# Where to undo a row permutation: in the output store, or in a copy on the way

## The chip, the cores and the metric

The kernel runs on one core of one Trainium2 chip. The metric is the device time in microseconds of one execution; of several executions the median is given. Beside it there is a profile of one execution, which names each instruction by its engine, its source line and the tiles that it reads and writes.

## What is computed

The reference is an attention with a small mask, followed by a feed-forward layer with a maximum of three projections in place of an activation function. All inputs and the output are fp32.

```python
B, H, S, D = 4, 8, 768, 64                  # batch, heads, tokens, head width
scores = q @ k.transpose / sqrt(D)          # keep: the last 96 positions, and the first 8 keys
scores = where(keep, scores - slope[h] * dist, -1e9)
attn   = softmax(scores) @ v                # (4, 8, 768, 64)

x   = attn.transpose(0, 2, 1, 3).reshape(3072, 512)
h   = max(x @ w1, x @ w2, x @ w3)           # 512 -> 768
out = h @ w_out                             # (3072, 512)
```

The kernel cuts the 3072 tokens into 24 tiles of 128 (tile T; six to a batch). Since a query sees only the 96 positions before it, a tile of queries needs its own tile of keys and the one before.

## The kernel before

The whole kernel is one hand-written order of small units, held in a string. A word such as `F0.1.0` calls a unit with its numbers. Each engine works through its own instructions in the order in which the words issue them, and waits where an input is not there yet or a buffer is not free.

- `T` (`u_XT`): the attention result of one tile is transposed, so that the feed-forward layer can multiply it. In `T1.1` the last number says how: 0 copies with ScalarE, 1 with VectorE, 2 with GpSimd, 4 transposes with a DMA.
- `F` (`u_F1`): one of the three up-projections (last number) of one 128-wide block of the hidden width for one chunk of tiles.
- `O` (`u_F2`): the down-projection of one tile (`O0.1.0` is chunk 0, second tile of it, copy by ScalarE) and the store of its 128 output rows.
- `X`: the transpose of queries and keys of one tile (`X18.4` by a DMA); `S`: scores; `A`: probabilities times values; `W`: cast of a weight block; `K`: a mask from an exponential.

The chunks are tiles 0-1, 2-3, 4-5, 6-7, 8-11, 12-15, 16-19, 20-23.

For an early start, the first four tiles of batch 0 are loaded in a way of their own: a partition takes four successive tokens, so that each read is longer. The queries of these tiles stay in that order. Within such a tile, row `e*32 + i` holds the token `4*i + e`. The order runs through scores, probabilities, attention result and feed-forward layer, and the output store of these tiles undoes it:

```python
    copies = (nc.scalar.copy, nc.vector.tensor_copy, nc.gpsimd.tensor_copy)
    # ... cut ...
    def u_XT(T, how):
        # ... cut: xT, the destination of the chunk ...
        dst = xT[B][:, :, lo:lo + 128]                      # [128, 4, 128] bf16
        if how == 4:
            nc.sync.dma_start_transpose(out=dst, in_=xb[T].rearrange("p h d -> p (h d)"))
            return
        if early(T):                                        # T < 4
            tp = psH.tile([128, NP, 128], BF16, name="xtp", tag="h")
        else:
            tp = psT.tile([128, NP, 128], BF16, name="xtp", tag="tp")
        x = xb[T].rearrange("p h d -> p (h d)")
        for jp in range(NP):
            nc.tensor.transpose(tp[:, jp], x[:, jp * 128:(jp + 1) * 128], identb)
        copies[how](dst, tp)

    def u_F1(c, f, j):
        # ... cut ...
        ps = psH.tile([128, W], FP32, name="h", tag="h")    # psH has three buffers
        for dm in range(4):
            nc.tensor.matmul(ps, w123[f // 2][:, dm, j, (f % 2) * 128:(f % 2) * 128 + 128],
                             xT[B][:, dm, o], start=(dm == 0), stop=(dm == 3))
        # ... cut: h01s[c, f] ...
        if j == 0:
            nc.scalar.copy(h01, ps)
        elif j == 1:
            nc.vector.tensor_max(h01, h01, ps)
        else:
            nc.vector.tensor_max(ht[B][:, f, o], h01, ps)

    def f2_out(po, c, tt, copy, cols=slice(0, DM), dma=nc.sync):
        T = chunks[c][tt]
        ost = ost_pool.tile(list(po.shape), FP32, name="ost", tag="ost")
        copy(ost, po)
        rows = out[T * 128:(T + 1) * 128, cols]
        dma.dma_start(out=rows.rearrange("(i e) c -> e i c", e=4) if T < 4 else rows, in_=ost)
```

Another unit, `u_x`, copies transposed queries and keys and has the same choice between a straight and a strided copy (lines 256 and 259 of the kernel):

```python
            if n == 0 and a == 0:
                copy(batch_T(0)[:, 0, j0 + lo:j0 + hi, 0:sz * 128].rearrange("c j (e i) -> c j e i", e=sz),
                     tp.rearrange("c e j i -> c j e i"))
            else:
                copy(dst[:, lo:hi], tp.rearrange("c e j i -> c j i e"))
```

All loads, DMA transposes and nearly all stores are issued by the sync engine, in the order of the schedule. Two parts of the string that matter below:

```
    ... s1.2.0 T0.0 C2.1.2 G3.2 C3.1.1 w0.0.0 W0.0.0 K4 T1.1 V1.2
    W0.1.1 A2.1 V2.2 A3.0 T2.0 F0.0.0 T3.1 V3.2 F0.0.1 w1.0.0 W1.0.2 W2.0.0 F0.1.0 F1.0.0 F1.1.0 F1.4.0
    # ... cut ...
    O3.0.1 F4.0.0 A12.0
    T12.4 F4.2.0 F4.2.1 S13.1 M13.1 S13.0 G12.2 F4.0.1 F4.1.0 F4.1.1 F4.1.2 G13.2 S14.0 C13.1.2 M13.0
    S14.1 M14.1 G14.1 M14.0 F4.4.0 F4.4.1 O0.0.0 C14.1.1 S15.1 M15.1 S15.0 G15.0 F4.4.2 C16.0.2 F4.3.0
    F4.3.1 A13.0 V13.1 T13.4 C19.0.1 F4.2.2 M15.0 O0.1.0 A14.0 V14.1 X18.4 X19.4 F4.3.2 O1.0.1 C15.1.2
    A15.0 T15.4 F4.0.2 F4.5.0 X16.4 T14.0 C17.1.1 L17 L20 F4.5.1 F4.5.2 O4.2.0 v19 O4.1.1 S18.0 S18.1
    M18.1 F5.0.0 C18.1.0 F5.1.0 S19.0 S16.1 ...
```

Of the kernel before, what the change touches and what calls it, by code (L numbers as in the profile page):

```python
# [25 lines left out]
    l0.5 c0.5.1 l0.0 D5.28 K5 D3.9 x0.5.3 l0.4 c0.4.1 K7 K1 g2.1.2 c0.0.0 K6 x0.0.2 x0.4.0 D2.9 g2.0.0  # L26
    s0.0.0 g1.0.1 l0.2 c0.2.2 l0.7 l0.1 c0.7.1 c0.1.1 K3 l0.6 c0.6.2 s1.0.1 v1 l0.3 x0.1.1 s0.1.0 x0.2.1
    g1.1.2 c0.3.2 x0.6.3 s0.2.1 x0.3.3 C1.1.2 g1.2.1 x0.7.2 s0.3.1 g2.3.0 v0 s1.1.0 C0.1.2 A0.2 w0.1.0
    v2 K0 g1.3.2 s1.3.1 G0.2 A1.2 v3 g2.2.2 s1.2.0 T0.0 C2.1.2 G3.2 C3.1.1 w0.0.0 W0.0.0 K4 T1.1 V1.2
    W0.1.1 A2.1 V2.2 A3.0 T2.0 F0.0.0 T3.1 V3.2 F0.0.1 w1.0.0 W1.0.2 W2.0.0 F0.1.0 F1.0.0 F1.1.0 F1.4.0  # L30
    F1.1.1 w0.2.0 l1.0 c1.0.2 F1.2.0 F0.4.0 W0.2.1 F1.0.1 F1.1.2 F0.1.1 F0.0.2 F1.3.0 x1.0.4 F1.0.2 l1.1
    F1.5.0 c1.1.2 x1.1.4 F0.2.0 w1.1.0 W1.1.2 F0.3.0 S4.1 K2 S4.0 G4.2 W2.1.1 F0.1.2 F1.5.1 M4.1 F1.4.1
    S5.1 F0.4.1 M4.0 M5.1 F0.2.1 F0.3.1 S5.0 v4 C4.1.2 A4.1 F0.5.0 F0.5.1 F1.2.1 w1.2.0 W1.2.0 W2.2.2
# [28 lines left out]
def kernel(  # L62
# [122 lines left out]
    copies = (nc.scalar.copy, nc.vector.tensor_copy, nc.gpsimd.tensor_copy)  # L185
# [49 lines left out]
    def early(T):  # L235
        return T < NSTART
# [152 lines left out]
    def u_XT(T, how):  # L389
        c, i = where[T]  # L390
        B = BIG[c]
        if B not in xT:
            xT[B] = xT_pool.tile([128, NP, WBIG[B]], BF16, name="xT", tag="xT")
        lo = OFF[c] + i * 128
        dst = xT[B][:, :, lo:lo + 128]
# [3 lines that stand above are left out]
        if early(T):  # L399
# [3 lines that stand above are left out]
        x = xb[T].rearrange("p h d -> p (h d)")  # L403
        for jp in range(NP):
            nc.tensor.transpose(tp[:, jp], x[:, jp * 128:(jp + 1) * 128], identb)  # L405
        copies[how](dst, tp)

    ht = {}
    h01s = {}
# [31 lines left out]
    def f2_out(po, c, tt, copy, cols=slice(0, DM), dma=nc.sync):  # L441
        T = chunks[c][tt]
        ost = ost_pool.tile(list(po.shape), FP32, name="ost", tag="ost")
        copy(ost, po)  # L444
        rows = out[T * 128:(T + 1) * 128, cols]
        dma.dma_start(out=rows.rearrange("(i e) c -> e i c", e=4) if T < 4 else rows, in_=ost)

    def u_F2(c, tt, how):
        po = psH.tile([128, DM], FP32, name="po", tag="h")
        f2_mm(po, c, tt, range(NF))  # L450
        f2_out(po, c, tt, copies[how])

    def u_E():
        n = len(chunks[last])
        pos = [psH.tile([128, DM], FP32, name="po", tag="h") for _ in range(2)]
        for tt in range(2):
            f2_mm(pos[tt], last, tt, range(NF - 1))
        for tt in range(2):
            f2_mm(pos[tt], last, tt, [NF - 1])
            f2_out(pos[tt], last, tt, nc.scalar.copy)  # L460
        for tt in range(2, n - 1):
            po = psT.tile([128, DM], FP32, name="po", tag="tp")
            f2_mm(po, last, tt, range(NF))
            f2_out(po, last, tt, nc.scalar.copy)
        for lo, hi, copy, dma in ((0, 256, nc.scalar.copy, nc.sync), (256, 384, nc.vector.tensor_copy, nc.sync),
                                  (384, 512, nc.scalar.copy, nc.scalar)):
            po = psH.tile([128, hi - lo], FP32, name="po", tag="h")
            f2_mm(po, last, n - 1, range(NF), slice(lo, hi))
            f2_out(po, last, n - 1, copy, slice(lo, hi), dma)
# [35 lines left out]
    with tc.manual_schedule():  # L505
# [20 lines left out]
        for h in range(4, H):  # L526
# [14 lines left out]

        units = {"l": load_part, "v": load_v, "c": cast_part, "x": u_x, "L": load, "w": load_w, "o": load_wo, "C": cast, "X": u_X, "S": u_S, "s": u_s, "g": u_g, "M": u_M,
                 "A": u_A, "G": put_kg, "V": put_vg, "T": u_XT, "F": u_F1, "W": cast_w,
                 "K": u_K, "Q": cast_wo, "O": u_F2, "E": u_E, "D": u_D}
        for u in SCHEDULE.split():
# [34 lines left out]
```

## Time and profile before

The time is 192.82 us, the median of three executions (192.77 to 194.81). The profiled execution took 192.07 us; 190.3 us of it lie between its first and last instruction, and all times of the profile are counted from that first instruction.

| | busy us | share of the span | instructions |
|---|---|---|---|
| TensorE, matmuls (PE) | 172.1 | 90% | 1654 |
| VectorE (DVE) | 123.3 | 65% | 269 |
| ScalarE (ACT) | 103.8 | 55% | 166 |
| GpSimd (POOL) | 38.9 | 20% | 68 |

TensorE's mean granted clock is 0.980 of full speed. The DMA engines moved 36.06 MB, at a mean of 190 GB/s.

How to read the lines that follow: a line names a source line (L446), an engine, an operation, and tiles as output<-input. SPq is the sync engine's own issuing of DMAs: the length given there is the time it took to issue, and the time to landing is counted from the start of the issue until the data are there. A chain of work is followed back from the last instruction: at each step to what released it, or to the instruction before it on its engine. Of the 13 copies at L406, seven are on ScalarE (593 ns in the middle) and six on VectorE (420 ns).

### The profile page before, as it was taken

Reading aid. Unit: us, or ns where it says so; the run is one execution under the profiler, and the core shown is the slowest. Engines: PE = TensorE matmul, PEld = TensorE weight load, DVE = VectorE, ACT = ScalarE, POOL = GpSimd, SP = SyncE. Lnnn points to the kernel's source line nnn. Section 1 sums busy time; section 2 is a strip of 40 time slices with the busy share of each in tenths; the row PEclk is TensorE's granted clock in tenths of the full one; section 3 lists DMA queues with packets and bytes.
Section 4 is the critical chain, followed back from the end, with each engine's and each line's share of the span. In section 5 each row is a group of like instructions: output and inputs, shape, how many; then the busy total and the mean of one; then the engine's idle time right before and its main releaser. Section 6 shows DMA issues by size and latency. Waiting matters only on the chain.

```text
span 190.3 us, 4220 instructions
## 1 busy us (share of the span) xinstructions
PE 172.1 (90%) x1654; PEld 104.7 (55%) x1654; DVE 123.3 (65%) x269; ACT 103.8 (55%) x166; POOL 38.9 (20%) x68
## 2 busy tenths in 40 slices
PE   7669799899999999999997059999999999999992
PEld 7345588688888866444553024455445455444442
DVE  7355756994899997466974003989836985435620
ACT  4979948939787794467221118544465605232122
POOL 5343443722094024003100001310003100000000
PEclk9999999999999999999999759999999999999999
DMA  5999999999889899986969899599999511720006
GB/s 151 309 277 332 323 335 348 325 288 221 197 276 222 172 212 149 205 233 152 192 85 163 97 170 269 110 207 127 168 217 277 130 27 61 233 98 0 0 9 215
DMA packets 83668, 36.06 MB, mean 190 GB/s; under 512 B 68288, under 2 KB 78400, under 8 KB 83648
## 3 DMA queue, kind: packets, MB, share of 16 engines
q1 hardware_dynamic: 83504, 35.73, 81.4%
q8 instruction: 13, 0.21, 0.6%
q14 instruction: 7, 0.06, 0.1%
q10 hardware_dynamic: 144, 0.07, 0.1%
HBM read 25.17 MB, written 6.29 MB: 165 GB/s over the span
## 4 chain that ended last, share of the span: by engine, by line
PE 75%; DVE 9%; ACT 7%; DMA 5%; issue 2%; POOL 0%; ACTq 0%; POOLq 0%; DVEq 0%
PE h L418 45%; PE po L438 15%; PE sp L293 5%; DMA xT<-xb 4%; PE op L367 3%; DVE P L350 2%; PE tpp L251 2%; ACT P L333 2%; PE op L370 2%; ACT wmask L344 2%; PE xtp L405 1%; DMA out_dram<-ost 1%; DVE ht L431 1%; DVE h01s L429 1%; DVE xb L386 1%
## 5 line engine op out<-in xcount | busy, mean ns | idle before, releaser
L418 PE MATMUL h<-xT,w 128*128 128x256 bf16 (+1 forms) x576 | 103.8, 329 | 8.1 <-DMA xT<-xb 7.0
L418 PEld LDWEIGHTS <-w 128*128 128x128 bf16 x576 | 53.6, 98 | 43.9 <-DMA xT<-xb 7.2
L297 ACT ACTIVATE P<-sp 128x1024 bf16<-128x1024 f32 (+1 forms) x40 | 36.5, 960 | 16.5 <-PE sp L293 16.4
L438 PE MATMUL po<-wo,ht 128*128 128x512 bf16 (+2 forms) x156 | 33.4, 363 | 0.0
L429 DVE TENSOR_TENSOR h<-h,h 128x512 bf16<-128x512 bf16 x24 | 16.4, 684 | 24.5 <-PE h L418 11.9
L427 ACT CAST h<-h 128x512 bf16<-128x512 f32 x24 | 14.1, 587 | 30.2 <-PE h L418 30.0
L350 DVE TENSOR_TENSOR P<-P,wmask 128x1024 bf16<-128x1024 bf16 x34 | 25.2, 753 | 3.6 <-ACT P L297 3.5
L438 PEld LDWEIGHTS <-ht 128*128 128x128 bf16 x156 | 14.3, 98 | 15.1 <-DVE ht L431 0.2
L444 ACT COPY ost<-po 128x512 f32<-128x512 f32 (+2 forms) x17 | 9.4, 557 | 19.9 <-PE po L438 15.0
L431 DVE TENSOR_TENSOR ht<-h,h 128x512 bf16<-128x512 bf16 x24 | 16.3, 681 | 3.2 <-PE h L418 2.5
L367 PEld LDWEIGHTS <-P 128*128 128x128 bf16 x192 | 12.4, 97 | 3.5 <-issue 1.0
L386 DVE TENSOR_TENSOR xb<-op,rz 128x512 bf16<-128x512 f32 x19 | 13.1, 691 | 0.7
L367 PE MATMUL op<-va,P 128*128 128x65 bf16 x160 | 12.6, 193 | 0.2
L293 PE MATMUL sp<-qkT 64*128 64x128 bf16 x296 | 12.0, 218 | 0.9 <-DMA qkT<-qkb 0.9
L444 DVE COPY ost<-po 128x512 f32<-128x512 f32 (+1 forms) x9 | 5.8, 644 | 10.8 <-PE po L438 10.7
L429 DVE TENSOR_TENSOR h01s<-h01s,h 128x256 bf16<-128x256 bf16 x24 | 9.7, 415 | 4.5 <-PE h L418 2.5
L293 PEld LDWEIGHTS <-qkT 64*128 64x128 bf16 x296 | 8.4, 94 | 7.3 <-issue 5.4
L201 POOL CAST va<-rawv 128x512 bf16<-128x512 f32 x12 | 7.8, 652 | 20.9 <-DMA rawv<-in_v_dram 8.6
L427 ACT CAST h01s<-h 128x256 bf16<-128x256 f32 x24 | 8.8, 378 | 4.7 <-PE h L418 4.2
L370 PEld LDWEIGHTS <-P 128*128 128x128 bf16 x160 | 10.5, 97 | 1.2
L431 DVE TENSOR_TENSOR ht<-h01s,h 128x256 bf16<-128x256 bf16 x24 | 9.7, 416 | 2.1 <-PE h L418 1.5
L195 POOL CAST qkp<-rawp 128x1024 bf16<-128x1024 f32 (+1 forms) x10 | 9.7, 972 | 6.0 <-DMA rawp<-in_q_dram 3.0
(85 smaller groups left out, 159.9 us busy)
## 6 DMA issues: line engine op xcount, KB each, us to landing
rawv<-in_v_dram SPq DMA_DIRECT2D x24, 256.0 KB, 5.8
out_dram<-ost SPq DMA_DIRECT2D x23, 256.0 KB, 4.1
wst<-in_moe_w_dram SPq DMA_DIRECT2D x3, 1024.0 KB, 7.7
raw<-in_q_dram SPq DMA_DIRECT2D x12, 256.0 KB, 4.6
raw<-in_k_dram SPq DMA_DIRECT2D x12, 256.0 KB, 5.1
rawp<-in_q_dram SPq DMA_DIRECT2D x4, 512.0 KB, 8.6
rawp<-in_k_dram SPq DMA_DIRECT2D x4, 512.0 KB, 8.6
wst<-in_moe_w_dram SPq DMA_DIRECT2D x3, 512.0 KB, 7.1
```

The costliest lines, as they stand in the source:

```text
L293: nc.tensor.matmul(sp[:, hh, j2, ds], qT(T - ds, 1)[hsl, jp], qT(T, 0)[hsl, jp], start=True, stop=True, skip_group_check=True)
L297: nc.scalar.activation(P[:, :, 0:n], sp.rearrange("p a b d n -> p (a b) d n")[:, :, 0:n], AF.Exp, bias=0.0, scale=scale)
L350: nc.vector.tensor_mul(P, P, wmask[:, g, :, 1:3])
L367: nc.tensor.matmul(o, get_P(T, g, j2, hh, 0), heads(va[T])[:, h], start=True, stop=(t == 0), skip_group_check=True)
L370: nc.tensor.matmul(o, get_P(T, g, j2, hh, 1), heads(va[T - 1])[:, h], start=False, stop=True, skip_group_check=True)
L386: nc.vector.tensor_tensor(out=x4, in0=o4[:, :, :, 0:64], in1=rz[:, :, :, None].to_broadcast([128, 2, 4, D]), op=ALU.mult)
L418: nc.tensor.matmul(ps, w123[f // 2][:, dm, j, (f % 2) * 128:(f % 2) * 128 + 128], xT[B][:, dm, o], start=(dm == 0), stop=(dm == 3))
L427: nc.scalar.copy(h01, ps)
L429: nc.vector.tensor_max(h01, h01, ps)
L431: nc.vector.tensor_max(ht[B][:, f, o], h01, ps)
L438: nc.tensor.matmul(po, ht[BIG[c]][:, f, lo:lo + 128], wo[:, f, cols], start=(f == 0), stop=(f == NF - 1))
L444: copy(ost, po)
```

## The change

The order of rows is put right one stage earlier and no longer in the store. For tiles 0 to 3, the copy of the transposed attention result out of PSUM writes column `e*32 + i` to column `4*i + e`: it reads straight and writes with a step of four bf16 elements. From there on the tokens are in their natural order, and the store of these tiles writes its 128 rows in order, as all the other stores do. The copies of tiles 1 and 3, which VectorE made, go to ScalarE, where those of tiles 0 and 2 already are. Nothing else in the schedule is moved.

```diff
-    v2 K0 g1.3.2 s1.3.1 G0.2 A1.2 v3 g2.2.2 s1.2.0 T0.0 C2.1.2 G3.2 C3.1.1 w0.0.0 W0.0.0 K4 T1.1 V1.2
-    W0.1.1 A2.1 V2.2 A3.0 T2.0 F0.0.0 T3.1 V3.2 F0.0.1 w1.0.0 W1.0.2 W2.0.0 F0.1.0 F1.0.0 F1.1.0 F1.4.0
+    v2 K0 g1.3.2 s1.3.1 G0.2 A1.2 v3 g2.2.2 s1.2.0 T0.0 C2.1.2 G3.2 C3.1.1 w0.0.0 W0.0.0 K4 T1.0 V1.2
+    W0.1.1 A2.1 V2.2 A3.0 T2.0 F0.0.0 T3.0 V3.2 F0.0.1 w1.0.0 W1.0.2 W2.0.0 F0.1.0 F1.0.0 F1.1.0 F1.4.0
@@ u_XT
-        copies[how](dst, tp)
+        if T < 4:
+            copies[how](dst.rearrange("c j (i e) -> c j e i", e=4), tp.rearrange("c j (e i) -> c j e i", e=4))
+        else:
+            copies[how](dst, tp)
@@ f2_out
-        rows = out[T * 128:(T + 1) * 128, cols]
-        dma.dma_start(out=rows.rearrange("(i e) c -> e i c", e=4) if T < 4 else rows, in_=ost)
+        dma.dma_start(out=out[T * 128:(T + 1) * 128, cols], in_=ost)
```

## The prediction

> **What bounds the kernel now.** I read the chain that ended last first: 75% of its time is on TensorE, 9% on VectorE, 7% on ScalarE, 5% on DMA. A chain that is mostly TensorE can only be shortened where TensorE stood still, so I listed that chain in order of time and looked for a long piece that is no computation. There is one (columns: start us, length us, what):
>
> ```profile
> 98.85 1.73 PE h L418 x8
> 100.58 2.60 PE po L438 x12
> ...
> 103.20 0.35 DVE ost L444
> 103.56 7.84 DMA xT<-xb
> 111.39 0.05 issue
> ```
>
> The waits between 100 and 115 us give what TensorE lost there (total us, times, longest):
>
> ```profile
> PE h L418 <- DMA xT<-xb: 7.0, 1, 7.0
> ...
> PE sp L293 <- DMA qkT<-qkb: 0.9, 1, 0.9
> ```
>
> The 7.0 us are the wait of the first up-projection of the second four-tile chunk (schedule word F5.0.0) for the DMA transpose of tile 15 (T15.4). The 0.9 us are scores of tile 18 waiting for X18.4. All these DMAs are issued in order by one queue, that of the sync engine:
>
> ```profile
> 91.87 1.28 SPq L397 DMA_TRANSPOSE xT<-xb  x1
> 93.24 0.59 SPq L446 DMA_DIRECT2D out_dram<-ost  x1
> 93.93 1.35 SPq L397 DMA_TRANSPOSE xT<-xb  x1
> 95.38 1.81 SPq L446 DMA_DIRECT2D out_dram<-ost  x1
> 97.28 5.54 SPq L266 DMA_TRANSPOSE qkT<-qkb  x2
> 102.92 0.54 SPq L446 DMA_DIRECT2D out_dram<-ost  x1
> 103.56 1.26 SPq L397 DMA_TRANSPOSE xT<-xb  x1
> ```
>
> Laid beside the schedule string, these are T12.4, O0.0.0, T13.4, O0.1.0, X18.4 with X19.4, O1.0.1, T15.4. So all three stores in this stretch are stores of tiles 0 to 2, which the change touches; the fourth, O1.1.0, goes out near 78.6 us, where TensorE waits for nothing. T12.4, behind an ordinary store, landed 3.4 us after its issue. T13.4, behind O0.0.0, took 6.4; X18.4, behind O0.1.0, took 6.7; T15.4, behind O1.0.1, took 7.8. The DMA activity shows why. First 99 to 102.5 us, where the touched store O0.1.0 is draining, in 40 slices (busy share in tenths, then GB/s); below it 164 to 169 us, with ordinary stores:
>
> ```profile
> DMA  9221511222333223324222454568999999992223
> GB/s 88 85 59 41 79 26 18 88 88 94 117 94 94 94 56 82 99 99 143 94 94 94 129 132 129 152 164 208 249 313 269 249 214 146 135 88 76 67 76 105
> ```
> ```profile
> DMA  9995699983000799999999993000088989600000
> GB/s 344 328 393 180 158 225 223 213 188 56 2 0 0 279 360 426 344 377 393 361 410 360 426 360 99 0 0 0 0 311 328 442 328 442 230 17 0 0 0 0
> ```
>
> The permuted store plods at about 94 GB/s with two or three tenths of the engines busy, which is four of sixteen; an ordinary one bursts at 328 to 442. 256 KB at 94 GB/s is 2.8 us, against about 0.7 at 380.
>
> **What the skill says.** "DMA: Bandwidth & Descriptors", section on why a DMA increments its semaphore by 16, says that a transfer runs on the largest count up to 16 that divides the slowest dimension of both access patterns. The permuted destination has 4 as its slowest dimension (e), hence four engines; the straight one has 128, hence 16. The trace agrees: 0.30 of the engines at 92 GB/s from 99.4 to 101.2 us. The same page, on queues, rings and completion order, says that each engine consumes its ring in order, so whatever is issued later waits on those four engines; 6.4, 6.7 and 7.8 against 3.4 us to landing agree. "TensorE: Matmul & The Clock Gate", Part 1, says that an idle window of about 3.4 us halves the clock. The trace agrees in kind: granted clock 0.73 from 104.2 to 111.4 us and 0.83 in the 8.6 us after. "VectorE: DVE Perf Modes", on what auto-detection checks, wants step 1 on 16-bit data for the fast mode: the strided 128x512 copy at L259 takes 688 ns on VectorE against 420 at L406, and 590 on ScalarE against 596 there. That is why the strided copies are all put on ScalarE.
>
> **The change, part by part.**
> (1) *Stores.* Four stores keep their 256 KB and 2 KB rows but go to sixteen engines. I re-time the queue. O0.1.0 takes 0.55 us to issue rather than 1.81: done at 95.95. X18.4 and X19.4 take 1.3 each, as undisturbed ones do, rather than 3.0 and 2.4: done at 98.6. O1.0.1's copy ends near 97.1 (VectorE, start 96.45), so its store goes at 98.65 rather than 102.92. T15.4 has its input at 97.98, so it goes at 99.25 rather than 103.56; with 3.4 to 5 us to landing it is there at 102.7 to 104.3. X18.4 lands near 96.0+4.2 = 100.2. TensorE has other work to 103.18, then tile 18's scores for 0.26, and asks for T15.4 at about 103.45. So it waits from 0 to 0.8 us instead of 0.87+7.0: 7.1 to 7.9 us come out of the chain.
> (2) *Clock.* The first eight 512-column matmuls after the stall take 3.30 us, against 1.73 for eight at 98.85. Without a long stall 1.5 us come out too.
> (3) *The copies, early.* Two VectorE copies of 0.42 (T1, T3) become ScalarE copies of 0.60, and T0 and T2 become strided. ScalarE is full there, 4.79 us of the 5 from 20 to 25. In its order T1.0 comes after the weight cast and the mask exponential:
>
> ```profile
> 20.12 1.08 ACT L494 CAST w<-wst 128x1024 bf16<-128x1024 f32 x1
> 21.07 0.91 ACT L344 ACTIVATE wmask<-rbase 128x384 bf16<-128x384 f32 x1
> 21.84 0.61 ACT L406 COPY xT<-xtp 128x512 bf16<-128x512 bf16 x1
> 22.31 0.42 ACT L427 CAST h01s<-h 128x256 bf16<-128x256 f32 x1
> 22.57 1.10 ACT L494 CAST w<-wst 128x1024 bf16<-128x1024 f32 x1
> ```
>
> So T1 runs at 21.85 to 22.45 (it ended at 19.52 on VectorE). The first up-projection F0.0.0 needs tiles 0 and 1 and moves from 21.53 to about 22.5; its ScalarE copy from 22.31 to about 23.15; then T3.0 until 24.05; then the cast W2.0.0 until 24.95, where it ended at 23.67. PSUM tag h has three buffers, so the fourth and fifth up-projections wait for ScalarE copies that start at 24.95 rather than 23.76. That is 0.9 to 1.2 us of delay, on a stretch where TensorE is the chain (22.85 to 28.58 without a break). VectorE's 0.84 us of relief saves nothing there. If writing every fourth element costs ScalarE more than reading with a stride does, four copies grow: for 0.4 us each, another 1.6. No row of the profile shows ScalarE writing such a stride into SBUF. L344, which reads SBUF fp32 with a stride, takes 871 ns for 384 elements, where 512 from PSUM take 596, so a penalty is possible.
> (4) *Sum.* 192.8 - 7.5 - 1.5 + 1.0 = 184.8. I add 0.9 for what comes back later: TensorE reaches the second half 8 us earlier, while the loads of tiles 17 and 20 (issued 107.6 to 113.0) come only some 5 us earlier, and VectorE is busy 8.83 us of the 10 from 120 to 130. Prediction 185.7.
>
> **Rivals.**
> *A: the stall moves rather than goes.* T15.4 now follows two large transposes and a store closely, and DMA is busy 0.9 to 1.2 of 16 engines' time around there; T15.4 may still land at 106, or tile 16's scores wait for X16.4. For it: X16.4 took 7.4 us, and the loads behind it queue. Against: the share counts queueing, and the bytes moved from 104.2 to 111.4 are only 91 GB/s. Half the gain would stay: 188 to 189.
> *B: the early loss wins.* The strided write costs 1.0 us a copy and ScalarE falls 2.5 us behind at 25 us, never recovered since TensorE is the chain thereafter. Against: ScalarE idles 0.5 us at 25.4 and 1.86 us before 28.62. With the full gain later: 187.
> *C: the stores are hidden and the landing times are the transposes' own.* Then only (3) is left: about 193.8. Against: T12.4 and later transposes land in 2.4 to 4.2 us with ordinary stores around, and the low GB/s.
> *D: all of the stall goes and the downstream follows in full:* 183.5.
>
> **Range and chances.** D and the sum with little given back span 183.5 to 186; A, or B in part, 187 to 189. I take 183.0 to 189.0. Faster by 2% means below 189.0; C and a strong A with B would miss it. Faster 0.87, same 0.11, slower 0.02.
>
> **What would show it.** In the profile after: transposes of tiles 13 and 15 and of 18 landing in 3 to 5 us; the SP queue issuing T15.4 near 100 us (plus the early delay); the wait of L418 on xT below 1 us; no dip of the clock near 105 to 115; the seven ScalarE copies at L406 become nine, and the six of VectorE four; F0.0.0 about 1 us later. The prediction is wrong if the touched stores still drain at about 94 GB/s, if T15.4 goes out early and yet lands 7 us later, or if strided copies of 1 us stand in the chain near 22 us.

## The result, and the profile after

The changed kernel takes 187.66 us (median; 186.5 to 188.19), the kernel before 193.72 us in the same measurement (192.77 to 194.81). The ratio is 0.968, with a 95% interval from 0.960 to 0.976. The prediction was 185.7 us in a range from 183.0 to 189.0.

In the profiled execution the span went from 190.3 to 184.7 us. Two things happened, of opposite sign. The stall near 104 us is gone:

Chain of work of the kernel after, in order of time (start us, length us, what):

```profile
100.49 1.73 PE h L421 x8
102.22 0.22 PE xtp L405 x4
102.44 1.73 PE h L421 x8
104.17 0.86 PE po L441 x4
105.03 0.05 issue
105.08 1.67 PE po L441 x7
106.75 0.33 PE sp L293 x8
107.08 1.83 PE h L421 x8
```

TensorE goes from the down-projections straight to the scores of tile 18 and to F5.0.0 (the last line, which stood at 111.44 us before). Its eight matmuls take 1.83 us, where they took 3.30 after the stall. The queue of the sync engine shows what let it go; the lines are T12.4, O0.0.0, T13.4, O0.1.0, X18.4 with X19.4, O1.0.1 and T15.4, in the same order as before:

```profile
92.42 1.25 SPq L397 DMA_TRANSPOSE xT<-xb  x1
93.77 0.71 SPq L448 DMA_DIRECT2D out_dram<-ost  x1
96.39 1.20 SPq L397 DMA_TRANSPOSE xT<-xb  x1
98.06 0.33 SPq L448 DMA_DIRECT2D out_dram<-ost  x1
98.48 2.67 SPq L266 DMA_TRANSPOSE qkT<-qkb  x2
101.25 0.53 SPq L448 DMA_DIRECT2D out_dram<-ost  x1
101.87 1.24 SPq L397 DMA_TRANSPOSE xT<-xb  x1
```

X18.4 and X19.4 are issued in 2.67 us together, not 5.54. T13.4 lands 2.4 us after its issue and T15.4 2.6, not 6.4 and 7.8. (T12.4, behind an ordinary store in both kernels, took 3.4 us before and 4.7 here.) The three stores themselves land in 3.9, 2.2 and 2.6 us; the profile of before gives no landing for them. T15.4 is there at 104.5 us, some 2.6 us before it is needed.

The other thing is early. ScalarE from 20 us on:

```profile
20.28 1.15 ACT L496 CAST w<-wst 128x1024 bf16<-128x1024 f32 x1
21.29 0.89 ACT L344 ACTIVATE wmask<-rbase 128x384 bf16<-128x384 f32 x1
22.05 2.46 ACT L407 COPY xT<-xtp 128x512 bf16<-128x512 bf16 x2
24.20 0.51 ACT L430 CAST h01s<-h 128x256 bf16<-128x256 f32 x1
24.57 1.35 ACT L407 COPY xT<-xtp 128x512 bf16<-128x512 bf16 x1
```

A strided copy takes 1.3 us and more; the straight one took 0.60. TensorE waits for it (waits from 18 to 30 us: total us, times, longest), and after that its clock drops. The first up-projection F0.0.0 and the run of 52 matmuls behind it, in the kernel before and then in the kernel after (the idle time of TensorE ahead of a line stands in brackets):

```profile
21.53 0.60 PE L418 MATMUL h<-xT,w 128*128 128x256 bf16 x4
22.69 5.89 PE L418 MATMUL h<-xT,w 128*128 128x256 bf16 x52
```
```profile
23.42 0.60 PE L421 MATMUL h<-xT,w 128*128 128x256 bf16 x4 [2.13 <-ACT xT L407]
24.56 7.68 PE L421 MATMUL h<-xT,w 128*128 128x256 bf16 x52 [0.32 <-ACT xT L407]
```

F0.0.0 starts 1.9 us later, and the run behind it takes 1.8 us longer. The stretch from 24.5 us in the table of stretches has, after the length and five engines' busy times, the granted clock, the DMA share and GB/s:

```profile
PE h L421 <- ACT xT L407: 2.5, 2, 2.1
```
```profile
24.50:25.50 1.00, 0.94 (x8) 0.76 (x8) 0.24 (x1) 1.00 (x3) 0.01 (x1) 0.82 0.89 185
25.50:26.50 1.00, 0.92 (x5) 0.52 (x4) 0.18 (x1) 1.00 (x2) 1.00 (x1) 0.50 1.07 375
26.50:27.50 1.00, 1.00 (x7) 0.67 (x6) 0.00 (x0) 0.90 (x3) 0.31 (x2) 0.50 1.05 393
27.50:28.50 1.00, 1.00 (x7) 0.67 (x6) 0.00 (x0) 0.37 (x1) 0.77 (x1) 0.50 1.16 329
```

What the clock falls short of full in these four microseconds adds up to 1.7 us. From there on the kernel runs late by much the same amount. A run of 20 up-projection matmuls, in the chain of before and of after, is 3.6 us later:

```profile
59.49 2.18 PE h L418 x20
```
```profile
63.08 2.18 PE h L421 x20
```

### The profile page after: what moved, and what is told of

It reads as the page before. It is cut to its first block, busy times and chain, and to the rows that moved or that the text cites. A ratio compares the mean times of both kernels' runs of the same rounds, so it can differ in the third digit from the quotient of the medians.

```text
span 184.7 us, 4205 instructions
## 1 busy us (share of the span) xinstructions
PE 171.3 (93%) x1639; PEld 105.2 (57%) x1654; DVE 121.9 (66%) x267; ACT 106.9 (58%) x168; POOL 39.3 (21%) x68
## 4 chain that ended last, share of the span: by engine, by line
PE 71%; ACT 11%; DVE 8%; DMA 4%; issue 2%; SPq 2%; POOL 0%; ACTq 0%; POOLq 0%; DVEq 0%
PE h L421 44%; PE po L441 14%; PE sp L293 5%; ACT xT L407 3%; DMA rawv<-in_v_dram 3%; ACT wmask L344 3%; PE op L367 2%; DVE P L350 2%; ACT P L333 2%; PE tpp L251 2%; PE op L370 2%; SPq L266 1%; DMA out_dram<-ost 1%; PE xtp L405 1%; DVE h01s L432 1%
## 5 line engine op out<-in xcount | busy, mean ns | idle before, releaser
L350 DVE TENSOR_TENSOR P<-P,wmask 128x1024 bf16<-128x1024 bf16 x34 | 25.7, 767 | 2.8 <-ACT P L297 2.6
L195 POOL CAST qkp<-rawp 128x1024 bf16<-128x1024 f32 (+1 forms) x10 | 10.6, 1079 | 5.3 <-DMA rawp<-in_q_dram 2.9
```

Of the source, the lines that this page charges most:

```text
L350: nc.vector.tensor_mul(P, P, wmask[:, g, :, 1:3])
```

## Experiments

The theory after this comparison: the stores of four tiles used four DMA engines and held up the queue behind them, which cost about 9.4 us; the strided write made four copies slow, which cost about 3.6 us. The rivals were that the scattered rows of the output are slow in themselves, that the move of two copies to ScalarE costs more than the stride, and that other parts of the change contribute. Each comparison has its own runs of the kernel before, whose median lay between 192.4 and 193.8 us. A measured time is a median with its lowest and highest execution; the ratio is that to the kernel before, with its 95% interval.

**The stores alone.** The copies stay straight, two of them on VectorE. The reordering is left out.

```diff
-        rows = out[T * 128:(T + 1) * 128, cols]
-        dma.dma_start(out=rows.rearrange("(i e) c -> e i c", e=4) if T < 4 else rows, in_=ost)
+        dma.dma_start(out=out[T * 128:(T + 1) * 128, cols], in_=ost)
```

> The kernel before with only its four stores in straight row order; the copies stay straight, tiles 1 and 3 stay on VectorE. Leaves out the reordering: the rows of the first four tiles come out permuted. Theory (the four-engine stores delay everything behind them on the queue, and that is the whole gain): the 7.9 us of waits near 103 to 111 us and the slow clock behind them go and nothing is lost early: 193.7 - 9 = 184.5 us, between 183 and 186. Rival (part of the gain comes from the copies leaving VectorE, or the stall moves elsewhere): 187 to 190 us.

Measured: 182.51 us (182.33 to 182.94), ratio 0.939 (0.933 to 0.945). In the profiles the span goes from 190.3 to 180.7, by 9.6 us. The run of 72 matmuls of the last chunk, in the chain of before and of this kernel in turn:

```profile
166.00 15.55 PE h L418 x72
```
```profile
156.45 15.54 PE h L418 x72
```

It moves by 9.55 us. The two waits (0.87 and 7.0) and the slow clock (1.57) make 9.4 of it, and nothing is given back. The stores are the whole gain. The median falls by 11.3 rather than 9.6, because the profiled execution of before, at 192.07 us, was one of its shorter ones. Executions of the kernel before differ by 2.5% (191.1 to 196.0 over all comparisons).

**The copies alone.** Strided writes on ScalarE, stores still permuted, so that the rows come out permuted twice.

> The kernel before with only the copies changed (strided writes, all four on ScalarE); the stores keep their permuted rows, so that the first four tiles come out permuted a second time. Theory (the early delay of 3.9 us seen at 41 us lies on the chain): 193.7 + 3.9 = 197.6 us, between 196 and 199. Rival (the later stall hides most of it, since the transpose of tile 15 waits for the store queue and not for TensorE): 194 to 195.5 us.

Measured: 197.19 us (197.02 to 198.35), ratio 1.016 (1.009 to 1.022), 3.4 us more than before. The stall swallows little of the delay:

```profile
107.34 8.05 DMA xT<-xb
```

T15.4 goes out at 107.34 instead of 103.56 and TensorE again waits 7.2 us for it, against 7.9 for both waits before. The store ahead of T15.4 and its input depend on TensorE, so they are late by nearly as much. The two halves do not quite add up: 11.3 us less by the stores and 3.4 more by the copies would be 7.9 less, where the changed kernel saved 6.1. With straight stores the copies cost 5.2 us by the medians (187.66 against 182.51, from two comparisons) and 4.0 by the profiled executions. Some 0.7 us of the difference is the shorter wait just named; where the rest comes from is not shown, and the kernel before spreads by more than that. The groups by form have the copies (count, then busy us and mean ns):

```profile
L407 ACT COPY xT<-xtp 128x512 bf16<-128x512 bf16 x4 | 5.1, 1352 | 0.1
L409 ACT COPY xT<-xtp 128x512 bf16<-128x512 bf16 x5 | 3.0, 591 | 1.0 <-PE xtp L405 1.0
```

**The move alone.** T1 and T3 copied by ScalarE, straight; stores as before.

```diff
-    ... K4 T1.1 V1.2 ... F0.0.0 T3.1 V3.2
+    ... K4 T1.0 V1.2 ... F0.0.0 T3.0 V3.2
```

> The kernel before with the copies of tiles 1 and 3 on ScalarE, straight as they were; stores permuted as before; the output is that of the reference. Theory (the stride makes the copies slow; the move alone costs what I had worked out): copies of 0.60 us, F0.0.0 about 1 us later, 193.7 + 1.0 = 194.7 us. Rival (the move alone makes the delay, the stride little): 196 to 198 us.

Measured: 193.99 us (192.92 to 195.83), ratio 1.004 (1.001 to 1.006). The copies take 602 ns. TensorE waits once for one of them, and its clock stays at 1.00 from 20 to 35 us:

```profile
PE h L418 <- ACT xT L406: 0.8, 1, 0.8
```

By the ratio the move costs some 0.7 us (0.2 to 1.2); the stride costs the rest of the early loss.

**The stride in the read.** The same permutation, with strided reads of PSUM (where the transposes by TensorE leave their result) and straight writes of SBUF (where xT lies).

```diff
-            copies[how](dst.rearrange("c j (i e) -> c j e i", e=4), tp.rearrange("c j (e i) -> c j e i", e=4))
+            copies[how](dst.rearrange("c j (i e) -> c j i e", e=4), tp.rearrange("c j (e i) -> c j i e", e=4))
```

> The changed kernel, with the same permutation made by reading PSUM with a stride and writing SBUF straight; all four copies still on ScalarE; the output is that of the reference. Theory (it is the write of every fourth bf16 element into SBUF that costs ScalarE 1.3 us): copies of 0.60 us, 187.7 - 2.9 = 184.8 us, between 183.5 and 186. Rival (any stride costs ScalarE the same): copies of 1.3 us, 187.7 us.

Measured: 183.32 us (183.17 to 184.23), ratio 0.944 (0.937 to 0.952), 4.3 us less than the changed kernel by one line.

```profile
L407 ACT COPY xT<-xtp 128x512 bf16<-128x512 bf16 x4 | 2.3, 616 | 0.0
```

The copy is back at 616 ns, TensorE waits 0.8 us for it instead of 2.1 and 0.3, the slow clock at 25 us is gone, and the gain of the stores is kept. It came out 1.5 us lower than expected and just under the range: I had counted only the shorter copies and not the slow clock (1.7 us).

**Sixteen engines, rows still scattered.** The kernel before with every permuted store cut into four DMAs of 32 rows.

```diff
-        dma.dma_start(out=rows.rearrange("(i e) c -> e i c", e=4) if T < 4 else rows, in_=ost)
+        if T < 4:
+            for e in range(4):
+                dma.dma_start(out=rows.rearrange("(i e) c -> e i c", e=4)[e], in_=ost[32 * e:32 * e + 32])
+        else:
+            dma.dma_start(out=rows, in_=ost)
```

> The kernel before, with each of the four permuted stores cut into four DMAs of 32 rows, one for each e: the rows still go to every fourth row of the output, but 32 is the slowest dimension of each; the output is that of the reference, the copies are straight. Theory (four engines at work is what makes these stores slow): they drain near 300 GB/s, the waits near 103 to 111 us go as with straight stores, less what three more issues a store cost the queue: 183 to 185.5 us. Rival (scattered rows in the output are slow in themselves): 191 us or more.

Measured: 184.07 us (183.71 to 184.78), ratio 0.954 (0.948 to 0.959). Every row goes to the same scattered place as before, and the stall is gone all the same. While O1.0.1's pieces go out, from 100.5 to 102.7 us, the DMA row shows bursts of up to 261 GB/s with pauses between, in place of a steady 94 or so. The 300 GB/s that I expected are not reached, but the transposes of tiles 13 and 15 land in 2.4 us each.

```profile
99.25 1.94 SPq L448 DMA_DIRECT2D out_dram<-ost  x4
101.28 1.19 SPq L397 DMA_TRANSPOSE xT<-xb  x1
```

**Four engines, rows in stretches.** The kernel before with each permuted store replaced by two DMAs with a slowest dimension of 4 and stretches of 16 rows in order. The reordering is left out.

```diff
-        dma.dma_start(out=rows.rearrange("(i e) c -> e i c", e=4) if T < 4 else rows, in_=ost)
+        if T < 4:
+            for x in range(2):
+                dma.dma_start(out=rows.rearrange("(a x r) c -> x a r c", a=4, x=2)[x], in_=ost[64 * x:64 * x + 64])
+        else:
+            dma.dma_start(out=rows, in_=ost)
```

> The kernel before, with each of its four permuted stores replaced by two DMAs whose slowest dimension is again 4, but which write stretches of 16 whole rows in order (32 KB each); copies straight. Leaves out the reordering: the rows of the first four tiles come out permuted. Theory (the slowest dimension of 4 is the cause, not the scatter): they drain near 94 GB/s and the stall is there: 192 to 195 us. Rival (the scatter is the cause): as with straight stores, 182.5 to 184 us.

Measured: 190.67 us (190.22 to 192.03), ratio 0.988 (0.982 to 0.995). Most of the stall is there, though the rows lie in order in stretches of 32 KB. From 98.2 to 100.7 us, with these stores draining, the DMA engines move 77 GB/s at a busy share of 0.35 (before, from 99 to 101.5 us: 102 and 0.40). In 40 slices:

```profile
DMA  3321701111341052213762513391224051636355
GB/s 123 103 66 33 131 33 66 66 66 66 131 131 66 33 131 98 98 37 74 139 106 8 74 41 53 53 111 41 37 45 90 4 82 37 70 102 98 70 139 135
```

TensorE's waits are 5.3 and 0.5 us rather than 7.0 and 0.9, and the time is 1.3 us under the range that the theory expected. For the longer wait the profile names no releaser:

```profile
PE h L418 <- issue: 5.3, 1, 5.3
```

It stands ahead of the same eight matmuls of F5.0.0, here at 109.45 us, and T15.4, whose landing this profile lacks, had been issued at 103.87; that it is the same wait is read from its place. So the count of engines is the main part. Whether the scatter has a share in the other 2 us, or the smaller DMAs, this run does not separate. Together with the split stores it rules out the scatter as the cause.

**Another queue.** The kernel before with its permuted stores issued by ScalarE's queue.

```diff
-        dma.dma_start(
+        (nc.scalar if T < 4 else dma).dma_start(
```

> The kernel before, with its four permuted stores issued by ScalarE's queue rather than the sync engine's; everything else as before, output that of the reference. Theory (the transposes suffer because they stand behind the stores in the same ring): the stores stay slow at some 94 GB/s, but the transpose of tile 15 lands in 3 to 5 us and is issued earlier: 183 to 187 us. Rival (four engines are slowed for everybody, whichever queue it is): the transposes of tiles 13 and 15 still take over 6 us, 190 to 194 us.

Measured: 188.66 us (187.25 to 190.39), ratio 0.980 (0.972 to 0.988), between the two. T15.4, now issued at 102.14, lands in 4.7 us. But X18.4 takes 9.2 us to land and X19.4 8.5, and the waits of TensorE are:

```profile
PEld L293 <- DMA qkT<-qkb: 2.6, 1, 2.6
PE sp L293 <- DMA qkT<-qkb: 2.2, 1, 2.2
PEld L293 <- issue: 1.3, 2, 0.8
PEld L418 <- DMA xT<-xb: 1.2, 1, 1.2
```

Both readings hold in part. Out of the stores' queue the last transpose is freed, but T12.4 (7.2 us to landing, 3.4 before) and the two large transposes crawl all the same; for T13.4 the profile has no landing. That they still need the four busy engines is the likely reason, and no run shows it by itself. A store on few engines harmed its neighbours here from another queue too.

**One store of four.** The kernel before with only the store directly ahead of T15.4 straight (tile 2, whose reordering is left out).

```diff
-        dma.dma_start(out=rows.rearrange("(i e) c -> e i c", e=4) if T < 4 else rows, in_=ost)
+        dma.dma_start(out=rows.rearrange("(i e) c -> e i c", e=4) if T in (0, 1, 3) else rows, in_=ost)
```

> The kernel before with only the store of tile 2 (O1.0.1, the one directly ahead of the transpose of tile 15) in straight row order; the other three stay permuted, all copies straight. Leaves out the reordering of tile 2. Theory (the stall has two parts: the queue is held up by the stores of tiles 0 and 1, so that the transpose of tile 15 is issued only near 103.5 us, and then it stands behind the store of tile 2): the issue stays near 103.5 us and the landing shortens from 7.8 to about 3 us, so that some 3 to 4 us of waiting remain: 187 to 189.5 us. Rival (only the last store matters): the stall goes nearly whole, 183 to 185 us.

Measured: 189.8 us (189.33 to 189.91), ratio 0.986 (0.981 to 0.990).

```profile
97.05 6.88 SPq L266 DMA_TRANSPOSE qkT<-qkb  x2
104.02 0.54 SPq L446 DMA_DIRECT2D out_dram<-ost  x1
104.65 1.27 SPq L397 DMA_TRANSPOSE xT<-xb  x1
```

T15.4 lands in 4.2 us instead of 7.8, but it is still issued at 104.65, since X18.4 and X19.4 behind the stores of tiles 0 and 1 take 6.88 us to issue. Waits of 3.4 and 1.5 us remain, and the time ends 0.3 us above the expected range. So the stall had two parts: T15.4 was held up before its issue, and again after it.

**The strided write on VectorE.** The changed kernel with T1 and T3 back on VectorE.

> The changed kernel with the copies of tiles 1 and 3 back on VectorE, still writing every fourth element; those of tiles 0 and 2 stay on ScalarE; output that of the reference. Theory (the slow strided write is ScalarE's own; VectorE only loses its fast mode): copies of 0.69 us on VectorE, 1.33 on ScalarE, half of ScalarE's early load gone: 184.5 to 186 us. Rival (a strided 16-bit write into SBUF is slow for any engine): 1.1 us or more on VectorE as well, 186 to 187.5 us.

Measured: 183.39 us (183.12 to 183.53), ratio 0.949 (0.944 to 0.955).

```profile
L407 ACT COPY xT<-xtp 128x512 bf16<-128x512 bf16 x2 | 2.6, 1319 | 0.0
L407 DVE COPY xT<-xtp 128x512 bf16<-128x512 bf16 x2 | 2.6, 1308 | 0.5 <-PE xtp L405 0.5
```

My theory of the copy fell: VectorE pays for this write as ScalarE does, 1.31 us, and not the 0.69 of a strided read. Yet the time is better than I expected from either. The slow copy costs little on VectorE, which has room there: TensorE waits 0.6 us, for the ScalarE copy, and the clock dip at 25 us does not come (1.00 from 20 to 35 us).

**A wider step.** The changed kernel, writing with a step of 32 elements; the rows come out in another wrong order.

```diff
+            copies[how](dst.rearrange("c j (e i) -> c j i e", e=4), tp.rearrange("c j (i e) -> c j i e", e=4))
```

> The changed kernel, with copies on ScalarE that read straight and write with a step of 32 elements (64 bytes) rather than 4 (8 bytes). Leaves out the right order: the rows of the first four tiles come out permuted another way. Theory (any strided write of bf16 into SBUF costs ScalarE the 1.3 us): copies of 1.3 us, 187 to 188 us. Rival (what is slow is to come back to the same few bytes often, at a step of 8): copies of 0.6 to 0.7 us, 183 to 184 us.

Measured: 192.22 us (190.98 to 192.97), ratio 0.995 (0.992 to 0.998). Both expectations missed: the copy takes 2.5 us.

```profile
L407 ACT COPY xT<-xtp 128x512 bf16<-128x512 bf16 x4 | 9.5, 2498 | 0.0
```

So strided writes differ among themselves: 1.35 us at 8 bytes, 2.5 us at 64, for the same 512 elements; the cost of the write is no constant. Why is open: with the step the inner run changes as well, from 32 elements to 4, and this run does not separate the two. It does set write against read. The strided read of above has the same step of 64 bytes and the same run of 4, on the side of PSUM, and takes 0.62 us. And four copies of 2.5 us eat nearly the whole gain of the stores.

**Better than both.** Strided reads, with T1 and T3 on VectorE:

> The changed kernel with the permutation made by strided reads of PSUM, and the copies of tiles 1 and 3 back on VectorE; output that of the reference. Theory (all that the change loses is ScalarE's time near 20 to 26 us; the stores' gain is kept whole): copies of 0.62 us on ScalarE and 0.69 on VectorE, first up-projection as early as before: 182.8 us, between 182 and 184, slightly under the version with all four on ScalarE (183.3). Rival (a floor set elsewhere): 183.3 again.

Measured: 182.74 us (182.49 to 183.01), ratio 0.947 (0.943 to 0.950). The copies take 610 ns on ScalarE and 692 on VectorE. This is within 0.25 us of the stores alone, which make no permutation at all, and 4.9 us under the changed kernel.

**The permutation in TensorE's identity.** The diff shows two of the places; the rest is cut.

```diff
+        nc.gpsimd.tensor_copy(identp.rearrange("p (i e) -> p i e", e=4), identf.rearrange("p (e i) -> p i e", e=4))
# ... cut: identp, its tile; tp in fp32 for T < 4; the straight store ...
-            nc.tensor.transpose(tp[:, jp], x[:, jp * 128:(jp + 1) * 128], identb)
+            if early(T):
+                nc.tensor.matmul(tp[:, jp], x[:, jp * 128:(jp + 1) * 128], identp, start=True, stop=True)
+            else:
+                nc.tensor.transpose(tp[:, jp], x[:, jp * 128:(jp + 1) * 128], identb)
```

> The kernel before with straight stores, where the permutation is made by TensorE: for the first four tiles the attention result is multiplied by an identity whose columns are permuted, into fp32, and all copies are straight (tiles 1 and 3 on VectorE); one copy on GpSimd builds that identity at the start; output that of the reference. Theory (a permutation in the matmul's moving operand costs nothing): matmuls as long as the transposes were, copies of 0.60 us on ScalarE and 0.69 on VectorE (it loses its fast mode on fp32): 182.8 us, between 182 and 184. Rival (the extra copy on GpSimd delays the start): 184 to 185 us.

Measured: 183.2 us (182.88 to 183.29), ratio 0.949 (0.945 to 0.952). The matmuls take 222 ns in the mean against 219 for the transposes, so the permutation there is free too, but it needs an extra tile and gains nothing over strided reads.

## Why the prediction was right, and where it was off

*What bounds the kernel; the four engines.* Right. The chain's long DMA piece was the place, and the link on which the rest hung, that the slowest dimension of 4 confines a store to four engines, as the Trainium skill says ("DMA: Bandwidth & Descriptors", on why a DMA increments its semaphore by 16), held by its effects: a slowest dimension of 32 takes the stall away with the rows where they were, and 4 with long stretches keeps most of it.

*(1) and (2), the stall and the clock.* Right in size: 7.5 and 1.5 us predicted, 7.9 and 1.5 measured (all of the waits of before; 3.30 us against 1.83 for the eight matmuls). The re-timed queue had T15.4 issued at 99.25 us; it was at 101.87, in a kernel that ran 3.6 us late, and landed in 2.6 us. With the stores alone it was at 98.57 and landed in 2.5. Rivals A and C fell with it.

*(3), the copies.* This is the term that was mis-sized: 1.0 us predicted, 3.6 measured. I had taken the strided write at 0.60 us, by analogy with strided reads at L259, and named a dearer write as a possibility worth another 1.6. It takes 1.32 to 1.35 us. The other part of the term, two copies moved to ScalarE, was about right: some 0.7 us with the move alone. F0.0.0 came at 23.42, 1.9 us later than before, and that in an execution that was 0.4 us ahead just earlier (the two exponentials ahead of these copies start in the chain at 17.56, against 17.96). TensorE's waits of 2.1 and 0.3 us were then followed by the slow clock, 1.7 us, which no step of mine had. 1.9 and 1.7 make the 3.6 (4.0 with the lead of 0.4). So rival B came true, and larger than I had drawn it, beside the full gain. One of my three signs of being wrong came true with it, the strided copies in the chain near 22 us:

```profile
22.18 2.33 ACT xT L407 x2
```

By that sign this step failed. The total stayed in the range because the range had room for B.

*(4), what comes back later.* 0.9 us predicted, about 0.2 measured. The loads moved forward with the queue and no later stage lost its lead; one wait on a load of v near 136 us is new in the chain.

The sum in the profiles: 9.4 gained, 3.6 lost early, 0.2 lost later, 5.6 in all, as the spans say. I had promised 7.1 (192.8 to 185.7): 2.6 too much for the copies, less 0.7 held back too much and 0.4 of stall too little, are the 1.5 between. That the smaller errors ran against the large one was luck.

## What to carry to other kernels

Before a DMA is reordered by its access pattern, look at its slowest dimension: one of 4 held these stores to about 94 GB/s, and the bill came at other DMAs around them, in late issues as well as in late landings. A row of DMA activity that sits at two or three tenths and a low GB/s was the sign of it here. When a permutation has to go into a copy from PSUM, try the stride on the side that is read (0.62 us here against 1.35), and the copy on the engine that has room at that time.

## What was not expected of the hardware

A 128x512 bf16 copy from PSUM to SBUF takes 0.60 us on ScalarE straight and 0.62 with a stride in the read; writing with a step of 8 bytes takes 1.35 us, with 64 bytes (and a shorter inner run) 2.5. VectorE, at 0.42 straight and 0.69 with a strided read, takes 1.31 for the write with 8 bytes, as long as ScalarE.

TensorE's clock fell to 0.50 near 25.5 us after waits of only 2.1 and 0.3 us with little work between. In the copies alone it was at 0.50 from 25 to 27 us after a single wait of 2.1 us; after waits of 0.6 to 0.8 us (the move alone, the strided reads, the write on VectorE) it stayed at 1.00. The Trainium skill ("TensorE: Matmul & The Clock Gate", Part 1) speaks of an idle window of about 3.4 us; the profile of the changed kernel shows no single idle stretch so long there.
